# A Mamba-2 scan feeding a float32 MLP on one core: decoding ahead of a lagging gate, and all scan scores in one group

## The chip, the cores and the metric

One core of one Trainium2 chip runs the kernel. The metric is device time in microseconds (us), the median of several executions. Five engines run at once, each with its own queue that is worked off in order: TensorE (PE in the profile, with its weight loads shown as PEld), VectorE (DVE), ScalarE (ACT), GpSimd (POOL) and SyncE (SP), which here only starts DMA transfers.

## What is computed

Two parts, one after the other. The first is a chunked state-space scan over `x` [4, 8, 768, 32] with decays `a` and projections `B` and `C` [4, 8, 768, 16]; per chunk and per (batch, head):

```python
cum = np.cumsum(la, axis=-1)                       # la = log(clip(a))
L = np.exp(cum[:, :, :, None] - cum[:, :, None, :]) * causal
CB = np.einsum('bhin,bhjn->bhij', Cc, Bc)          # the scores
y_intra = np.einsum('bhij,bhjd->bhid', CB * L, xc)
y_inter = np.einsum('bhin,bhnd->bhid', Cc, state) * decay_to_i[:, :, :, None]
state = decay_full * state + sum_j(Bx)             # carried to the next chunk
```

The second takes the scan's result as 3072 tokens of 256 values and computes `h = x @ w_in` (256 to 2048), `g = h * clip(h + 3, 0, 6) / 6` and `g @ w_out` (2048 to 256). The two weights arrive as float64, so the kernel decodes them to float32 on the chip.

## The kernel before

**Blocks and tiles.** The 768 steps are cut into NC = 6 blocks of 128 steps; with 4 batches a block has 512 tokens. Each block's MLP goes over NF = 16 tiles of 128 hidden units (f = 0 to 15). While the MLP of block k runs, the scan of block k + 1 is threaded between its tiles, since the next block's MLP needs its result.

**Block 0** uses the decoded weights directly in float32: per tile `first_full` (two products into a bank of PSUM, L654), `gate_full` (ACT L661, then DVE L662) and, five tiles later, `second` (four products with `Aacc`, L666; the same line serves all products of the helper `product`). Four PSUM banks (h0, h1, G0, G1) go round for the hidden tiles, so tile f + 4 needs that the gate of tile f has read its bank.

**Decoding** of a weight piece (eight pieces, four of each weight; `decode`) is five steps of a generator: (a) ACT copies the top 16 bits, L194; (b) DVE L211, L213, L197; (c) ACT L217; (d) ACT L219, DVE L201, and the load of a later piece; (e) DVE L225 and L231, which writes the piece `full`. The list `WEAVE` says which pieces take a step at tile f: in block 0 these steps stand in the DVE and ACT queues *behind* `gate_full(f)`.

**Blocks 1 to 5** split each float32 operand in two float32r parts and take three products each way. Per tile f: `follow` (four products, L666), `lead` of the next tile (two products, into the other of the banks h0, h1), `scale` (ACT L674, in place on that bank), `ramp` (ACT L701), `gate` (DVE L706), `g_high` (ACT L716), `g_low` (DVE L720), `g_gap` (POOL L725), and `second` of tile f - 2 (six products). The last two tiles of the last block take a float32 path of their own (`whole`, `gate_whole`, `second_whole`).

**Splitting the weights** into their parts (`split_w`, `split_o`; ACT L622/L641, DVE L624/L643, POOL L627/L646) happens piece by piece in blocks 0 and 1.

**The scan of one block**, in PE order: `into_state` (32 products, `sp`, L488), `scores` (`cb`, L477), `from_state` (L466) and `mix` (L536) into `yy`. A float32 product of these small shapes shows as two instructions in the trace. DVE multiplies the decays `L` with the scores (`weigh`, L509), `take` (ACT L504), `halfway` and `renew` (DVE L498, L525) form the state, and `y_high`, `y_gap`, `y_low` (ACT L602, DVE L605, L610) write the next MLP's input. Scores, `from_state` and `mix` are done in two rounds, one for each half of the heads (u = 0, 1), because all of them pass through the same pair of banks, "xy".

**Preparing the scan.** SP loads `B` and `C` as `pairs` (L90, 16 transfers), `x`, and the running sums for `L` and `eto`; POOL masks L (`conceal`, L156), adds (`add_cum`, L370), makes `bs` (`ends`, L390); DVE turns B and C (`turn_squares`, L439), and makes `cT` and `csT` (`part_heads` L446, `fade` L452). The block's output is turned by DVE (L768) and stored with 32 transfers (L774).

**Order.** It is written out by hand: `at(t, slot, fn, ...)` books work for step t = 16 k + f and a slot of that step (mid, ramp, gate, act, low, pool, late, pe, end), and the loop calls `go(t, slot)` at fixed places. Each engine's queue therefore has the order in which the loop meets the calls.

Of the kernel before, what the change touches and what calls it, by code (L numbers as in the profile page):

```python
# [8 lines left out]
FP32 = mybir.dt.float32  # L9
# [5 lines left out]
ALU = mybir.AluOpType  # L15
# [6 lines left out]
def kernel(  # L22
# [507 lines left out]
    def mix(c, u, start=(False, False), batches=range(NB)):  # L530
        xt = xts[c]
        for b in batches:
            for h in range(u * HU, (u + 1) * HU):
                for a, rows in enumerate(HALF):
                    d0 = D * (h % HU)
                    nc.tensor.matmul(  # L536
                        out=ys[c][a, u][d0:d0 + D, b], lhsT=xt[rows, b * NH + h],
                        rhs=Ls[c][rows, b, h], start=(start[a] and b == 0), stop=True,
                        tile_position=(a * HT, d0), skip_group_check=True)
# [11 lines left out]
    def mix_first():  # L551
# [3 lines left out]
        for u in range(2):  # L555
            mix(0, u, (u == 0, True))
# [10 lines left out]
    def scan_scores(c, u):  # L567
        cb = bank("cb", [2, NB, 2, HT], "xy")
        cbs[c] = {2 * u + t: cb[:, t] for t in range(2)}
        scores(c, (2 * u, 2 * u + 1))  # L570
# [3 lines left out]
    def added(c, batches):  # L574

        if c not in sps:
            both = bank("sp", [2, TB], "xy")
            sps[c] = [both[:, a, :NB * 2 * D].rearrange("p (b d) -> p b d", b=NB)
                      for a in range(2)]
        into_state(c, batches)  # L580

    def from_states(c, u):

        both = bank("yy", [2, TB], "xy")
        yall[c, u] = both[:, :, :NB * HT]
        ys.setdefault(c, {}).update(
            {(a, u): yall[c, u][:, a].rearrange("p (b i) -> p b i", b=NB) for a in range(2)})
        for a in range(2):
            from_state(c, a, (2 * u, 2 * u + 1), start=True)

    def own(c, u, batches):
        mix(c, u, batches=batches)
# [37 lines left out]
    def split_o(i):  # L630
# [15 lines left out]
        nc.gpsimd.tensor_tensor(out=lo_, in0=w, in1=hi_, op=ALU.subtract)  # L646
# [233 lines left out]
    def plan_turned(c, t):  # L880
        at(t, "low", turn_squares, bcs[c][1], turned(c)[0])
        at(t + 1, "low", turn_squares, bcs[c][0], turned(c)[2])
        at(t + 2, "gate", part_heads, c)
        at(t + 2, "low", fade, c)

    def plan_round(c, u, t):
        at(t, "pe", scan_scores, c, u)
        at(t + 1, "gate", weigh, c, (2 * u,))
        at(t + 1, "low", weigh, c, (2 * u + 1,))
        at(t + 2, "pe", from_states, c, u)  # L890
        at(t + 2, "pe", own, c, u, (0,))
        at(t + 3, "pe", own, c, u, range(1, NB))
        at(t + 4, "ramp", y_high, c, u)
        at(t + 4, "gate", y_gap, c, u)
        at(t + 4, "gate", y_low, c, u)

    def plan_scan(c, t):
        at(t, "mid", added, c, range(3))
        at(t + 1, "pe", added, c, range(3, NB))
        at(t + 2, "ramp", take, c)  # L900
        at(t + 2, "gate", halfway, c)
        plan_round(c, 0, t + 2)
        at(t + 5, "low", renew, c)
        plan_round(c, 1, t + 7)

    def plan_parts(gen, t):
        at(t, "act", next, gen)
        at(t + 1, "low", next, gen)
        at(t + 1, "late", next, gen)

    SPLITS = [split_w(0), split_o(0), split_w(1), split_w(2), split_o(1), split_w(3),
              split_o(2), split_o(3)]
    for n, gen in enumerate(SPLITS):
        plan_parts(gen, (10, 12, 14, 16, 18, 21, 23, 25)[n])


    WEAVE = ["1", "114", "44", "442", "22", "225", "55", "55", "33", "33", "36",
# [8 lines left out]
    at(4, "pe", turn, 1)  # L926
    at(5, "pe", added, 1, range(NB))
    at(6, "gate", take, 1)
    at(6, "gate", halfway, 1)
    for u in range(2):  # L930
        t = (6, 10)[u]
        at(t, "pe", scan_scores, 1, u)
        at(t + 1, "gate", weigh, 1, (2 * u, 2 * u + 1))
        at(t + 1, "pe", from_states, 1, u)
        at(t + 2, "mid", own, 1, u, range(2))
        at(t + 2, "pe", own, 1, u, range(2, NB))
        at(t + 3, "ramp", y_high, 1, u)
        at(t + 3, "gate", y_gap, 1, u)
        at(t + 3, "gate", y_low, 1, u)
    at(8, "low", renew, 1)  # L940
    at(5, "pe", load_bc, 2)
    at(6, "pe", rows, 2)
    at(10, "pe", load_x, 2)
    plan_factors(2, 9)
    for f in range(NF):
        first_full(f)
        go(f, "mid")
        go(f, "ramp")
        gate_full(f)
        go(f, "gate")  # L950
        for i in WEAVE[f]:
            weights(int(i), 1)
        go(f, "act")
        go(f, "low")
        go(f, "pool")
        go(f, "late")
        if f >= BEHIND:
            second(0, f - BEHIND)
        go(f, "pe")
# [5 lines left out]
    for k in range(1, NC):  # L965
        t0, c = NF * k, k + 1
        if c < NC:
            s0 = t0 + 2
            plan_scan(c, s0)
            if c + 1 < NC:  # L970
                at(t0, "pe", rows, c + 1)
                at(s0 + 2, "pe", load_bc, c + 1)
                at(s0 + 11, "pe", load_x, c + 1)
                s1 = s0 + NF
                plan_factors(c + 1, s1 - (7 if k < 2 else 9))
# [98 lines left out]
```

## Time and profile before

| What | Value |
|---|---|
| Median of 3 runs | 381.92 us (381.5, 381.92, 383.69) |
| The profiled execution: its own time / its span | 379.74 us / 377.3 us |
| Busy share of the span: PE, DVE, ACT, POOL | 92%, 66%, 60%, 49% |
| Mean granted TensorE clock | 0.984 |
| Chain that ended last: PE, DVE, ACT, POOL | 65%, 16%, 8%, 4% |
| Costliest wait: POOL L725 for DVE gl L720 | 98.7 us in 54 waits |
| DMA moved | 25.13 MB, mean 67 GB/s |

Span is the time from the first to the last instruction; 2.4 us lie around it. Matmuls are pipelined, so a busy PE is not a PE at its peak: what a tile costs is read from the distance between equal instructions of one tile and the next. Groups in the profile name what is written, then what is read (`Aacc<-g,full`), and a line number of the kernel.

### The profile page before, as it was taken

The numbers are of one execution on the slowest core, as the hardware profiler recorded it, in microseconds if no ns is written. First come the engines' busy times: TensorE is split into PE (matmuls) and PEld (weight loads), VectorE is DVE, ScalarE is ACT, GpSimd is POOL, SyncE is SP. The second block draws the span as 40 slices with busy tenths as digits, with TensorE's granted clock in tenths as the row PEclk, the third lists the DMA queues.
The fourth block names the chain that finished last, engine by engine and source line by source line (L and its number), as shares of the span: only waits on it lengthen the run. The fifth ranks groups of instructions, "written<-read, shape, count | busy, mean of one in ns | idle before, by whom it ended". The sixth has DMA issues, their size and how long they took to land.

```text
span 377.3 us, 7999 instructions
## 1 busy us (share of the span) xinstructions
PE 347.7 (92%) x3148; PEld 241.9 (64%) x3148; DVE 250.8 (66%) x370; ACT 226.5 (60%) x388; POOL 184.7 (49%) x157
## 2 busy tenths in 40 slices
PE   6796889899997989879999999999999999999995
PEld 2552344433565757647777877777877777878882
DVE  6768667877388797786465785574867664465442
ACT  4676545687475655665556765465765555666661
POOL 2303001480466769984349954369844243445440
PEclk9999599999999999999999999999999999999998
DMA  7999466555001241900241911243201100002101
GB/s 162 213 269 204 132 142 149 128 70 126 0 3 22 33 67 35 181 5 11 33 60 40 169 30 20 34 65 64 21 2 30 28 2 3 0 7 32 20 0 56
DMA packets 94180, 25.13 MB, mean 67 GB/s; under 512 B 86784, under 2 KB 90528, under 8 KB 93632
## 3 DMA queue, kind: packets, MB, share of 16 engines
q1 hardware_dynamic: 89760, 23.33, 32.4%
q10 hardware_dynamic: 4384, 1.31, 1.5%
q8 instruction: 24, 0.39, 0.4%
q14 instruction: 12, 0.10, 0.1%
HBM read 21.33 MB, written 3.29 MB: 65 GB/s over the span
## 4 chain that ended last, share of the span: by engine, by line
PE 65%; DVE 16%; ACT 8%; POOL 4%; issue 4%; DMA 3%; SPq 0%; ACTq 0%; DVEq 0%; POOLq 0%
PE h L666 24%; PE Aacc L666 20%; PE Gacc L666 7%; PE h L654 5%; DVE gl L720 3%; PE cb L477 3%; PE yy L466 3%; POOL gg L725 2%; DVE g L706 2%; ACT gh L716 2%; PE yy L536 2%; ACT g L661 2%; DMA raw<-in_moe_w_in_dram 2%; ACT g L701 1%; DVE full L231 1%
## 5 line engine op out<-in xcount | busy, mean ns | idle before, releaser
L725 POOL TENSOR_TENSOR gg<-gh,gl 128x512 fp32r<-128x512 f32 x78 | 108.5, 1391 | 108.7 <-DVE gl L720 98.7
L701 ACT ACTIVATE g<-h,ramp_bias 128x512 f32<-128x512 f32 x78 | 53.7, 688 | 69.1 <-PE h L666 68.2
L720 DVE SCALAR_TENSOR_TENSOR gl<-gh,g 128x512 fp32r<-128x512 f32 x78 | 64.3, 824 | 42.8 <-ACT gh L716 38.9
L706 DVE SCALAR_TENSOR_TENSOR g<-g,h 128x512 f32<-128x512 f32 x78 | 53.3, 683 | 46.8 <-ACT g L701 46.4
L716 ACT ACTIVATE gh<-g 128x512 fp32r<-128x512 f32 x78 | 49.3, 633 | 36.8 <-DVE g L706 36.4
L666 PE MATMUL Aacc<-gh,oparts 128*128 128x512 f32 x156 | 62.0, 397 | 1.9 <-DVE stage L762 1.8
L666 PE MATMUL Gacc<-gg,oparts 128*128 128x512 f32 x156 | 61.6, 395 | 1.1 <-POOL gg L725 0.9
L666 PE MATMUL Aacc<-gl,low 128*128 128x512 f32 x156 | 61.1, 392 | 1.5 <-POOL low L646 1.5
L666 PE MATMUL h<-yp,w_high 128*128 128x512 f32 x160 | 54.1, 419 | 0.1
L666 PE MATMUL h<-yp,w_gap 128*128 128x512 f32 x160 | 51.1, 400 | 1.9 <-DVE g L706 1.9
L666 PE MATMUL h<-yp,low 128*128 128x512 f32 x160 | 49.9, 393 | 0.0
L674 ACT ACTIVATE h<-h 128x512 f32<-128x512 f32 x80 | 47.2, 591 | 0.0
L666 PE MATMUL Aacc<-g,full 128*128 128x512 f32 x72 | 36.0, 628 | 4.3 <-DVE full L231 4.3
L156 POOL TENSOR_SCALAR_AFFINE_SELECT L<-L 64x1024 f32<-64x1024 f32 (+1 forms) x16 | 22.0, 1378 | 29.6 <-DMA L<-cum_d 29.2
L666 PEld LDWEIGHTS h<-yp,w_gap 128*128 128x128 f32 x160 | 29.7, 188 | 10.5 <-DVE g L706 3.5
L666 PEld LDWEIGHTS Aacc<-gh,oparts 128*128 128x128 f32 x156 | 29.3, 188 | 9.4 <-DVE stage L762 2.7
L666 PEld LDWEIGHTS Gacc<-gg,oparts 128*128 128x128 f32 x156 | 29.3, 188 | 9.1 <-POOL gg L725 2.4
L666 PEld LDWEIGHTS Aacc<-gl,low 128*128 128x128 f32 x156 | 29.3, 188 | 8.5 <-POOL low L646 1.9
L666 PEld LDWEIGHTS h<-yp,low 128*128 128x128 f32 x160 | 30.0, 188 | 7.1
L666 PEld LDWEIGHTS h<-yp,w_high 128*128 128x128 f32 x160 | 27.6, 188 | 9.5 <-issue 2.3
L654 PE MATMUL h<-y,full 128*128 128x512 f32 x64 | 32.3, 637 | 1.1 <-DVE full L231 1.1
L666 PEld LDWEIGHTS Aacc<-g,full 128*128 128x128 f32 x72 | 14.0, 201 | 21.4 <-issue 17.5
(121 smaller groups left out, 411.9 us busy)
## 6 DMA issues: line engine op xcount, KB each, us to landing
raw<-in_moe_w_out_dram SPq DMA_DIRECT2D x4, 1024.0 KB
L<-cum_d SPq DMA_DIRECT2D x8, 512.0 KB
xt<-in_x_dram SPq DMA_DIRECT2D x6, 512.0 KB
raw<-in_moe_w_in_dram SPq DMA_DIRECT2D x3, 1024.0 KB
out_dram<-back SPq DMA_DIRECT2D x160, 16.0 KB
pairs<-in_C_dram SPq DMA_DIRECT2D x40, 32.0 KB
eto<-cum_e SPq DMA_DIRECT2D x20, 64.0 KB
B<-in_B_dram SPq DMA_DIRECT2D x5, 256.0 KB
```

Of the source, the lines that this page charges most:

```text
L156: nc.gpsimd.affine_select(out=t[rows], in_=t[rows], pattern=pattern, compare_op=ALU.is_ge, fill=-1e5, base=base, channel_multiplier=-1)
L466: nc.tensor.matmul(out=ys[c][a, q // 2][d0:d0 + 2 * D, b], lhsT=state[pair, b], rhs=csT[pair, b, HALF[a]], start=(start and b == 0), stop= ...
L477: nc.tensor.matmul(out=cbs[c][q][rows, b], lhsT=bT[pair, b, rows], rhs=cT[pair, b, :, rows], start=(b == 0), stop=True, tile_position=(32 ...
L536: nc.tensor.matmul(out=ys[c][a, u][d0:d0 + D, b], lhsT=xt[rows, b * NH + h], rhs=Ls[c][rows, b, h], start=(start[a] and b == 0), stop=True ...
L654: nc.tensor.matmul(out=h, lhsT=full[f // FP][:, j, f % FP * P:(f % FP + 1) * P], rhs=yps[0][:, j], start=(j == 0), stop=(j == NK - 1))
L666: nc.tensor.matmul(out=out_, lhsT=w, rhs=y, start=start, stop=True, skip_group_check=True)
L674: nc.scalar.mul(hs[k, f], hs[k, f], -1.0 / UP)
L701: nc.scalar.activation(g, hs[k, f], AF.Relu, bias=ramp_bias, scale=UP * UP / 6.0 / Z)
L706: nc.vector.scalar_tensor_tensor(out=g, in0=g, scalar=UP / Z, in1=hs.pop((k, f)), op0=ALU.min, op1=ALU.mult)
L716: nc.scalar.mul(gs[k, f][1], g, CUT * Z)
L720: nc.vector.scalar_tensor_tensor(out=low_, in0=high, scalar=-1.0 / Z, in1=g, op0=ALU.mult, op1=ALU.add)
L725: nc.gpsimd.tensor_tensor(out=gap, in0=high, in1=low_, op=ALU.subtract)
```

## The change

The words given with the change are: block 0 decodes ahead of a gate lagging a step; all scores in four banks at once; C and B turned by VectorE; last two tiles' second product in float32. Of these, `turn_squares` and the `whole` path stand in the kernel before as well; the diff moves the first in time and does not touch the second.

1. **Block 0.** The loop now runs to f = 16; at step f the decode steps of `WEAVE[f]` stand ahead of the gate of tile f - 1. `WEAVE` begins one step earlier.
2. **Scores.** All four pairs of heads are scored at once, into two banks of the hidden tiles and the two of "xy". In block 0 these are G0 and G1, at step 9. In blocks 1 to 4 there is one special step, f = 6: no `lead` of the next tile ahead of it, then gate, `second` of tile 4, all scores in banks h1 and h0, the four `weigh`, `second` of tile 5, then `lead` and `scale` of tiles 7 and 8.
3. **The rest of the scan.** `own` does `from_state` and `mix` in two groups, the first for half 0 of the steps with heads u = 0 and half 1 with u = 1, the second crosswise; a tiny ACT copy (`settle`) stands between them. `into_state` is no longer cut in two.
4. **Bookings.** Turning C and B moves from steps 14, 15, 16 to 11, 12, 13, and the masks and decays with them; `load_x` to step 9; in block 1 the stores of block 0 move from steps 3, 4 to 11, 14.
5. **Splits.** The last operation of `split_o(2)` and `split_o(3)` moves from POOL to DVE, and several splits are booked a step or two later.

```diff
-    def mix(c, u, start=(False, False), batches=range(NB)):
+    def mix(c, us, start=(False, False)):
...
+                    u, h, d0 = us[a], us[a] * HU + n, D * n
...
+    def all_scores(c, *tags):
+        own_ = [bank("cb", [NB, 2, HT], t) for t in tags]
+        both = bank("cb2", [2, NB, 2, HT], "xy")
+        cbs[c] = own_ + [both[:, t] for t in range(2)]
+        scores(c, range(NQ))
...
+    def own(c, us):
...
+        for a, u in enumerate(us):
+            from_state(c, a, (2 * u, 2 * u + 1), start=(us == (0, 1)))
+        mix(c, us)
...
+    def settle(c):
+        nc.scalar.copy(out=spare, in_=yall[c])
...
-        nc.gpsimd.tensor_tensor(out=lo_, in0=w, in1=hi_, op=ALU.subtract)
+        engine = nc.vector if i > 1 else nc.gpsimd
+        engine.tensor_tensor(out=lo_, in0=w, in1=hi_, op=ALU.subtract)
...
+    def plan_scan(c, t, slot, e):
+        at(t, slot, added, c)
+        at(t + 1, "ramp", take, c)
+        at(t + 1, "gate", halfway, c)
+        at(t + 2, "low", renew, c)
+        special[e] = c
+        at(e + 1, "pe", own, c, (0, 1))
+        at(e + 2, "ramp", settle, c)
+        at(e + 3, "pe", own, c, (1, 0))
+        plan_y(c, e + 4)
+    for gen, t, u, v in (
+            (split_w(0), 10, 11, 11), (split_o(0), 12, 13, 13), (split_w(1), 14, 15, 15),
+            (split_w(2), 16, 17, 17), (split_o(1), 18, 20, 20), (split_w(3), 21, 23, 23),
+            (split_o(2), 22, 24, 25), (split_o(3), 25, 28, 29)):
...
-    WEAVE = ["1", "114", "44", "442", "22", "225", "55", "55", "33", "33", "36",
+    WEAVE = ["114", "144", "4", "422", "22", "225", "55", "55", "33", "33", "36",
...
+    at(9, "mid", all_scores, 1, "G0", "G1")
+    at(9, "gate", weigh, 1, range(NQ))
+    at(10, "pe", own, 1, (0, 1))
+    at(11, "ramp", settle, 1)
+    at(12, "pe", own, 1, (1, 0))
+    plan_y(1, 13)
...
+    for f in range(NF + 1):
+        if f < NF:
+            first_full(f)
+            go(f, "mid")
+            for i in WEAVE[f]:
+                weights(int(i), 1)
+        if f:
+            gate_full(f - 1)
...
-                at(s0 + 2, "pe", load_bc, c + 1)
-                at(s0 + 11, "pe", load_x, c + 1)
-                s1 = s0 + NF
-                plan_factors(c + 1, s1 - (7 if k < 2 else 9))
+                at(t0 + 4, "pe", load_bc, c + 1)
+                at(t0 + 9, "pe", load_x, c + 1)
+                plan_factors(c + 1, t0 + 10)
...
-            at(t0 + 3 + m, "low", store, k - 1, m)
+            at(t0 + (11 + 3 * m if k == 1 else 3 + m), "low", store, k - 1, m)
...
-                plan_turned(c + 1, s1 - 4)
+                plan_turned(c + 1, t0 + 11, t0 + 12, t0 + 13)
...
+            skip = t in special
+            if skip:
+                ramp(k, f)
+                gate(k, f)
...
+                second(k, f - 2)
+                scan = special.pop(t)
+                all_scores(scan, *(f"h{(f + n) % 2}" for n in (1, 2)))
+                weigh(scan, range(NQ))
+                g_gap(k, f)
+                second(k, f - 1)
+                for n in (1, 2):
+                    lead(k, f + n)
+                    scale(k, f + n)
```

## The prediction, made before the changed kernel was run

> **What bounds the kernel now.** I read the page's busy shares first, then the sums by stage, cut at the first `follow` of each block (97.4, 159.0, 215.6, 269.5, 322.9 us), then the timeline inside the slow stages. Columns: length; busy us of PE, PEld, DVE, ACT, POOL; PE clock; DMA share; GB/s.
>
> ```profile
> 22.60:97.40 74.80, 66.23 (x451) 30.14 (x451) 52.90 (x74) 46.46 (x76) 19.74 (x15) 0.93 0.66 135
> 97.40:159.00 61.60, 55.77 (x510) 40.31 (x509) 47.94 (x57) 37.61 (x68) 43.87 (x29) 1.00 0.30 49
> 159.00:215.60 56.60, 53.98 (x513) 41.04 (x512) 37.92 (x54) 34.48 (x60) 37.86 (x35) 1.00 0.30 51
> 215.60:269.50 53.90, 53.16 (x513) 41.41 (x512) 35.31 (x55) 33.59 (x58) 34.44 (x30) 1.00 0.29 46
> 269.50:322.90 53.40, 52.67 (x511) 41.01 (x511) 33.48 (x54) 31.36 (x54) 23.06 (x19) 1.00 0.07 11
> 322.90:377.30 54.40, 49.50 (x210) 38.24 (x208) 26.46 (x42) 30.74 (x53) 19.97 (x16) 0.98 0.10 20
> ```
>
> PE sets the pace in blocks 3 and 4: a plain tile takes 2.78 us (the chain of waits has equal products at 213.01 and 215.79), 16 of them 44.4 us, and the scan's inserts the other 9.5. Blocks 1 and 2 are 7 and 2.7 us longer for the same work. Block 0 is 74.8 us long with 8.6 us of idle PE, and part of it ran at half clock:
>
> ```profile
> 38.00:42.00 4.00, 3.75 (x4) 1.18 (x4) 2.12 (x6) 2.94 (x5) 0.00 (x0) 0.50 0.58 223
> 42.00:46.00 4.00, 3.27 (x67) 2.10 (x68) 3.96 (x5) 2.49 (x3) 0.00 (x0) 0.50 0.23 19
> ```
>
> Why PE waits there (the timeline of all engines: start, us, engine, line; in brackets the idle time before and its releaser):
>
> ```profile
> 34.00 0.69 DVE L662 SCALAR_TENSOR_TENSOR g<-g,h 128x512 f32<-128x512 f32 x1 [1.25 <-ACT g L661]
> 34.61 1.32 DVE L201 SCALAR_TENSOR_TENSOR wm<-raw,wm 128x1024 f32<-128x1024 uint32 x1
> 35.85 0.90 DVE L225 TENSOR_TENSOR wse<-wse 128x1024 uint16<-128x1024 uint16 x1
> 36.78 1.32 DVE L231 SCALAR_TENSOR_TENSOR full<-wm,wse 128x1024 f32<-128x1024 f32 x1
> 38.24 3.75 PE L666 MATMUL Aacc<-g,full 128*128 128x512 f32 x4 [2.85 <-DVE full L231]
> ```
>
> The decode (L201 to L231) stands behind a gate that waits for its own product; PE then waits 2.85 us for the weight, and its next four products take 3.75 instead of 1.72 us.
>
> **Block 0.** PE's work by rows: 30 groups of four products at 1.72 (16 first, 14 second) 51.6; `lead` 0.5, turning 0.9, `sp` 1.1, scores 2 x 1.03, `from_state` 2 x 1.07, `mix` 4 x 0.38, eight switches at 0.1: 60.6. So 14.2 us are lost, about 4.0 of them to the half clock. In the new order I laid the queues side by side with these rows (L194, L217, L219 about 1.07 each; L211 to L197 1.5; L201 and L231 1.2; L225 0.7; gate halves 0.69). Piece 1 is ready at 28.3 instead of 30.8, but the gate of tile 0 now stands behind three decode steps of piece 4 and ends at 31.4: tile 4, which takes its bank, waits 1.8 us. Piece 4 is ready at 35.2 (before 38.1), its tile waits 0.3. Piece 2 is ready at 41, piece 5 at 49, piece 3 at 60, all ahead of need; pieces 6 and 7 (70, 81) are just in time. The loads behind them come earlier, since each waits for an L201: 35.99 to about 33, 44.42 to 38.6. New waits: the scores at step 9 need bank G1, which the gate of tile 7 leaves at 52.5 (1.5 us), and tile 10 needs G0, free when the first `weigh` is done (0.8). With 0.2 more, 4.6 us of waits. The scores' group falls from 2.06 to 1.13 us:
>
> ```profile
> 14.74 1.20 PE L477 MATMUL cb<-cT,bT 32*64 32x128 f32 x64 [1.94 <-DVE cT L446]
> ...
> 177.93 1.10 PE L477 MATMUL cb<-cT,bT 32*64 32x128 f32 x32 [0.51 <-ACT gh L716]
> ```
>
> The first scan already scores all four pairs at once, 64 instructions in the time of 32. Block 0: 60.6 - 0.9 + 4.6 = 64.3 for 74.8: **-10.5**. The longest wait is 1.8 us, so I count no half clock. Without that cover: +4.0.
>
> **Blocks 1 to 4, the inserts.** Before, from tile distances above 2.78: `sp` 1.17 + 0.37 + 0.1; scores 1.81 + 1.13 + 0.2; `yy` 2 x 2.38; together 9.5. After: `sp` in one group 1.45. The special step costs 1.13 + 0.1 for the scores, 0.36 for the gate of tile 6 (ramp, gate, two hand-overs 1.75 us, under a `second` of 1.39), and 0.45 for `scale` of tile 7 (0.59 plus hand-overs, under a `lead` of 0.47): 2.05. Four `weigh` (2.6) end before `own` needs them. `own` 2 x (1.07 + 0.87 + 0.2). `settle` is bounded by 0 and 0.4 (the `adds` copy, L504, 0.37) on an ACT that is idle 40%; I take 0. Together 7.8: **-1.75 per block**.
>
> **Blocks 1 to 3, what the bookings add.** The turning of C and B now meets the `y` work: steps 10 to 13 have no insert on PE to cover it, 11.1 us, and DVE gets 2.8 (two gate halves, two y parts) + 3.85 (the same and a turn, 1.09) + 2.45 + 3.1 (two cT 1.0, fade 0.68) = 12.2. And the turned tile must have landed:
>
> ```profile
> 229.84 15.91 SPq L774 DMA_DIRECT2D out_dram<-back  x32
> 245.85 0.40 SPq L83 DMA_DIRECT2D B<-in_B_dram  x1
> 246.29 6.70 SPq L90 DMA_DIRECT2D pairs<-in_C_dram  x8
> 253.03 4.62 SPq L90 DMA_DIRECT2D pairs<-in_B_dram  x8
> ```
>
> On SP's queue the 32 stores of a block, first issued 4.6 us into tile 3, stand ahead of B and C; the last packet lands 29.5 us after the first store (259.4). In blocks 2 and 3 that is 44 us after the block's start (tile 3 at 9.8, + 4.6 + 29.5); tile 11 begins at 38.4 (11 x 2.78 + 7.8) and DVE gets to the turn 4.6 later, at 43.0. It waits about 0.9, all gates behind it wait too, `lead` of tile 14 starts 0.9 late, the next two 0.4 and 0.2; 0.5 more for POOL, whose masks and adds (20 us of work with its L725 in six tiles of 16.7) are in the same steps. **+2.0 each.** In exchange block 2 loses its old 2.7 us of waits (turning and `fade` at 161 to 167). Block 2: 53.9 - 1.75 + 2.0 = 54.15 for 56.6, **-2.45**; block 3 54.15 for 53.9, **+0.25**; block 4, which prepares nothing, **-1.75**. In block 1 the stores go behind the loads, so B and C are early, but their turns (0.70 each) and `split_o(3)` (1.22 and 1.2) join DVE: steps 10 to 13 hold 15.2 us, and the last part of piece 7 comes 3.9 after tile 12's `second` wants it. With 0.8 for POOL and 0.5 at tile 4: 53.9 + 0.66 (two float32 seconds) - 1.75 + 5.2 = 58.0 for 61.6: **-3.6**. Block 5 and the tail: 0.
>
> Moving two `low` operations from POOL (L646, 2.37 alone) to DVE has a price on both: a DVE instruction with two SBUF inputs and a POOL instruction take turns:
>
> ```profile
> 134.82 1.21 DVE L643 SCALAR_TENSOR_TENSOR oparts<-oparts,full 128x1024 fp32r<-128x1024 f32 x1
> ...
> 135.06 2.12 POOL L725 TENSOR_TENSOR gg<-gh,gl 128x512 fp32r<-128x512 f32 x1 [2.98 <-DVE gl L720]
> ```
>
> L725 takes 1.30 alone and 2.12 here. The two moved operations may each wait out one L725 (0 to 1.3); I take 0 and keep 2.6 as a rival. [...]
>
> **Sum.** -10.5 - 3.6 - 2.45 + 0.25 - 1.75 = -18.05. The profiled execution's own 379.74 becomes 361.7 (span 359.25); it lies 0.57% under the median, so on 381.92 the forecast is **363.9 us**.
>
> **Rivals.** (A) Blocks 1 to 3 run clean: C and B land sooner or DVE has slack; -9 of the 9.2 charged: **354.9**. For it: their waits hang on margins of about 1 us. (B) ACT, not DVE, holds block 0: at step 10 it waits for `eto` and the mask of L (landing at about 62.6 by the old distances), and the gates behind it are late; half the idle stays, +6: **369.9**. (C) The moved splits wait for POOL: +2.6, **366.5**. (D) The clock halves again. One PE gap of 2.85 us gave 10.24 us at 0.5; dense tiles lose 5.1 in that. If the gap stays in block 0 (+4.0) and the DVE waits of blocks 1 to 3 each come as one gap over 2.85 (+15.3), it ends at **383.2, slower**. It decides from gaps near 2.85; I reckon with 0.9 to 1.8, only block 1 is near. [...] (E) The change does less than it says: in banks shared with hidden tiles the 64 scores run as slowly as two groups, 5 x 0.93: **368.5**; the first scan speaks against it.
>
> **Numbers.** Forecast 0.56, A 0.18, B 0.11, C 0.07, D 0.05, E 0.03. The forecast's own spread is 359 to 369; the range takes in A and B: 353.5 to 372. About 0.5% (1.9 us) is what a measurement here can tell from no change: faster 0.92, same 0.03, slower 0.05.
>
> **What would show it.** Right: no 0.50 in PE's clock around 38 to 47; no wait of PE for `full` over 0.5 us but a wait of tile 4 for a gate; `cb` x64 in 1.1 to 1.2 us; block 0 near 64, blocks 2 and 3 near 54, block 4 near 51.7; DVE's `bT` waiting for `pairs` in blocks 2 and 3. Wrong: gaps of PE moved to step 10 of block 0 (B), blocks 2 and 3 at 52 (A), any new 0.50 (D).

## The result, and the profile after

| | Before | After |
|---|---|---|
| Median (4 runs each, one session) | 382.37 us (381.5 to 383.69) | 378.24 us (377.65 to 379.16) |
| Ratio after / before, 95% interval | | 0.9891 [0.9855, 0.9928] |
| Profiled execution: own time / span | 379.74 / 377.3 us | 378.26 / 376.5 us |

The kernel is faster by about 1.1%, where 4.7% was forecast; 378.24 us lies outside the range of 353.5 to 372. The stages show where the rest went. This is the sum by stage of the changed kernel, cut again at the first `follow` of each block (columns as in the prediction):

```profile
23.60:91.10 67.50, 61.16 (x449) 28.57 (x450) 54.81 (x72) 45.88 (x77) 19.08 (x15) 0.97 0.74 149
91.10:160.00 68.90, 58.18 (x510) 42.42 (x509) 51.64 (x63) 38.11 (x70) 44.22 (x32) 0.93 0.17 25
160.00:215.00 55.00, 52.58 (x514) 40.03 (x512) 36.34 (x54) 33.11 (x59) 30.76 (x28) 1.00 0.49 87
215.00:270.10 55.10, 52.68 (x513) 40.16 (x513) 36.92 (x55) 33.17 (x59) 33.70 (x30) 1.00 0.25 35
270.10:322.60 52.50, 51.46 (x513) 40.57 (x514) 32.43 (x50) 32.16 (x57) 25.34 (x22) 1.00 0.08 11
322.60:376.50 53.90, 49.05 (x207) 37.81 (x205) 26.09 (x41) 30.47 (x52) 19.41 (x15) 1.00 0.10 20
```

Block 0 won 7.3 of the 10.5 us forecast. Block 1 **lost** 7.3 us (61.6 to 68.9) where 3.6 were to be won: it is now the longest stage, with 10.7 us of idle PE and a mean clock of 0.93. Blocks 2 to 4 are each 0.9 above the forecast. From here on line numbers are those of the changed kernel: L663 `first_full`, L670/L671 `gate_full`, L675 `product`, L715 `gate`, L725 `g_high`, L729 `g_low`, L734 `g_gap`; L632 and L635 are the DVE and POOL operations of `split_w`, L651 and L655 the last two of `split_o`.

**Block 0.** The old gap at 35.4 us is gone, and so is the half clock behind it. A new gap stands late in the block (timeline of all engines):

```profile
65.17 0.63 ACT L384 ACTIVATE eto<-eto 128x512 f32<-128x512 f32 x1 [8.23 <-DMA eto<-cum_e]
68.39 0.69 DVE L671 SCALAR_TENSOR_TENSOR g<-g,h 128x512 f32<-128x512 f32 x1 [5.98 <-ACT spare L600]
70.37 3.20 POOL L635 TENSOR_TENSOR w_gap<-w_high,low 128x1024 fp32r<-128x1024 f32 x1 [3.91 <-DVE low L632]
71.27 2.85 DVE L225 TENSOR_TENSOR wse<-wse 128x1024 uint16<-128x1024 uint16 x1
74.16 1.32 DVE L231 SCALAR_TENSOR_TENSOR full<-wm,wse 128x1024 f32<-128x1024 f32 x1
75.53 0.94 PE L675 MATMUL Aacc<-g,full 128*128 128x512 f32 x1 [2.78 <-DVE full L231]
```

ACT waits 8.23 us for `eto` to land; the gates and the decode of piece 6 stand behind it in ACT's queue, so DVE idles 5.98 us (a gate waits for several things, and the one named last, L600, is a copy of 0.14 us that stood in ACT's late queue itself). L225 then runs beside GpSimd and takes 2.85 us (0.68 at 40.29), and PE waits 2.78 us for the decoded weight.

**Block 1.** Most of the loss is in tile 6, the special step: 13.20 us, against 7.58 in blocks 2 and 4. The same view there:

```profile
112.42 2.35 POOL L655 TENSOR_TENSOR low<-full,oparts 128x1024 fp32r<-128x1024 f32 x1
112.66 2.66 DVE L729 SCALAR_TENSOR_TENSOR gl<-gh,g 128x512 fp32r<-128x512 f32 x1 [0.76 <-ACT gh L725]
114.82 0.50 PE L675 MATMUL Aacc<-gl,low 128*128 128x512 f32 x1 [2.46 <-POOL low L655]
115.69 1.51 DVE L498 SCALAR_TENSOR_TENSOR state<-adds,parity,later 128x128 f32<-128x128 f32 x2
117.13 0.67 DVE L715 SCALAR_TENSOR_TENSOR g<-g,h 128x512 f32<-128x512 f32 x1
117.86 1.55 PE L477 MATMUL cb<-cT,bT 32*64 32x128 f32 x43 [1.25 <-DVE g L715]
```

GpSimd's `low` of `split_o(1)`, now booked for step 20, ends at 114.8; PE has wanted it for 2.46 us. DVE's `g_low` beside it takes 2.66 us instead of 0.69 (such a stretching beside GpSimd is called the lock from here on), `renew` (L498) stands behind that, the gate of tile 6 behind `renew`, and the scores, which take the gate's bank, wait another 1.25 us. Then the clock (windows of 3.4 us):

```profile
113.40:116.80 3.40, 1.79 (x7) 1.04 (x7) 3.37 (x3) 0.75 (x2) 2.67 (x2) 1.00 0.26 59
116.80:120.20 3.40, 2.34 (x63) 2.01 (x64) 1.98 (x5) 1.58 (x2) 0.78 (x1) 0.50 0.09 22
120.20:123.60 3.40, 3.40 (x9) 2.63 (x9) 2.19 (x4) 0.00 (x0) 0.49 (x1) 0.50 0.00 0
```

After a stretch in which PE was busy 1.79 of 3.40 us it runs at 0.50 for 6.83 us. Tile 10 has a wait of 1.56 us (for the `low` of `split_o(2)`), tile 14 waits of 1.31 and 2.43 us (a gate; the `low` of `split_o(3)`), and 3.41 us at half clock:

```profile
154.51 0.80 PE L675 MATMUL Aacc<-gl,low 128*128 128x512 f32 x1 [2.43 <-DVE low L655]
```

**The rest.** All 64 score instructions take 1.21 us (at 53.83), as forecast. Behind a block's stores the order on SP's queue is as before, and `bT` follows 30.2 us after the first store (first SP's queue, the stores and the last of `pairs`):

```profile
229.14 16.59 SPq L783 DMA_DIRECT2D out_dram<-back  x32
...
252.33 4.62 SPq L90 DMA_DIRECT2D pairs<-in_B_dram  x8
```

And DVE's timeline, the turn that reads it, after 0.66 us of idle time whose releaser the trace does not name:

```profile
259.33 1.11 DVE L439 STREAM_TRANSPOSE bT<-pairs 128x512 f32<-128x512 f32 x1 [0.66 <-issue]
```

### The profile page after: what moved, and what is told of

It is laid out like the page before. It is cut to its first block, busy times and chain, and to the rows that moved or that the text cites. A ratio compares the mean times of both kernels' runs of the same rounds, so it can differ in the third digit from the quotient of the medians.

```text
span 376.5 us, 8016 instructions
## 1 busy us (share of the span) xinstructions
PE 343.1 (91%) x3148; PEld 240.0 (64%) x3148; DVE 255.5 (68%) x372; ACT 225.2 (60%) x393; POOL 178.3 (47%) x155
## 3 DMA queue, kind: packets, MB, share of 16 engines
q10 hardware_dynamic: 4384, 1.31, 1.6%
## 4 chain that ended last, share of the span: by engine, by line
PE 36%; SPq 7%; DVE 7%; ACT 4%; DMA 2%; issue 2%; POOL 1%; ACTq 0%; POOLq 0%; DVEq 0%
PE h L675 16%; PE Aacc L675 11%; PE Gacc L675 5%; SPq L783 4%; SPq L90 3%; DVE g L715 2%; DMA L<-cum_d 2%; DVE gl L729 2%; ACT gh L725 1%; DVE cT L446 1%; ACT g L710 1%; PE yy L466 1%; POOL gg L734 1%; PE yy L537 1%; DMA pairs<-in_B_dram 1%
## 5 line engine op out<-in xcount | busy, mean ns | idle before, releaser
L734 POOL TENSOR_TENSOR gg<-gh,gl 128x512 fp32r<-128x512 f32 x78 | 107.5, 1379 | 120.0 <-DVE gl L729 112.1
L729 DVE SCALAR_TENSOR_TENSOR gl<-gh,g 128x512 fp32r<-128x512 f32 x78 | 63.7, 816 | 47.2 <-ACT gh L725 42.5
L725 ACT ACTIVATE gh<-g 128x512 fp32r<-128x512 f32 x78 | 49.3, 631 | 56.1 <-DVE g L715 55.2
L715 DVE SCALAR_TENSOR_TENSOR g<-g,h 128x512 f32<-128x512 f32 x78 | 53.2, 681 | 42.8 <-ACT g L710 42.5
L710 ACT ACTIVATE g<-h,ramp_bias 128x512 f32<-128x512 f32 x78 | 53.4, 685 | 44.3 <-PE h L675 44.1
L675 PE MATMUL Aacc<-gl,low 128*128 128x512 f32 x156 | 62.7, 402 | 6.5 <-DVE low L655 4.0
L675 PE MATMUL Aacc<-gh,oparts 128*128 128x512 f32 x156 | 62.7, 402 | 1.0 <-ACT stage L763 0.7
L675 PE MATMUL Gacc<-gg,oparts 128*128 128x512 f32 x156 | 62.7, 402 | 0.0
L675 PE MATMUL h<-yp,w_gap 128*128 128x512 f32 x160 | 51.2, 406 | 4.3 <-DVE g L715 4.3
L675 PE MATMUL h<-yp,w_high 128*128 128x512 f32 x160 | 53.2, 413 | 1.4 <-ACT h L683 1.0
L675 PE MATMUL h<-yp,low 128*128 128x512 f32 x160 | 50.3, 396 | 0.0
L675 PEld LDWEIGHTS h<-yp,w_gap 128*128 128x128 f32 x160 | 30.0, 191 | 15.0 <-DVE g L715 7.8
L675 PEld LDWEIGHTS Aacc<-gl,low 128*128 128x128 f32 x156 | 29.8, 191 | 14.4 <-DVE low L655 4.9
L675 PE MATMUL Aacc<-g,full 128*128 128x512 f32 x72 | 35.1, 619 | 3.2 <-DVE full L231 3.2
L675 PEld LDWEIGHTS h<-yp,w_high 128*128 128x128 f32 x160 | 28.7, 190 | 13.4 <-ACT h L683 6.1
L675 PEld LDWEIGHTS Aacc<-gh,oparts 128*128 128x128 f32 x156 | 29.7, 190 | 9.5 <-ACT stage L763 1.1
L675 PEld LDWEIGHTS h<-yp,low 128*128 128x128 f32 x160 | 30.2, 189 | 7.0
L675 PEld LDWEIGHTS Gacc<-gg,oparts 128*128 128x128 f32 x156 | 29.9, 191 | 6.5
L663 PE MATMUL h<-y,full 128*128 128x512 f32 x64 | 30.2, 604 | 1.5 <-DVE g L671 1.4
L156 POOL TENSOR_SCALAR_AFFINE_SELECT L<-L 64x1024 f32<-64x1024 f32 (+1 forms) x16 | 20.0, 1252 | 24.5 <-DMA L<-cum_d 24.0
L675 PEld LDWEIGHTS Aacc<-g,full 128*128 128x128 f32 x72 | 13.7, 194 | 19.7 <-issue 15.2
```

The source lines that it names most:

```text
L156: nc.gpsimd.affine_select(out=t[rows], in_=t[rows], pattern=pattern, compare_op=ALU.is_ge, fill=-1e5, base=base, channel_multiplier=-1)
L663: nc.tensor.matmul(out=h, lhsT=full[f // FP][:, j, f % FP * P:(f % FP + 1) * P], rhs=yps[0][:, j], start=(j == 0), stop=(j == NK - 1))
L675: nc.tensor.matmul(out=out_, lhsT=w, rhs=y, start=start, stop=True, skip_group_check=True)
L710: nc.scalar.activation(g, hs[k, f], AF.Relu, bias=ramp_bias, scale=UP * UP / 6.0 / Z)
L715: nc.vector.scalar_tensor_tensor(out=g, in0=g, scalar=UP / Z, in1=hs.pop((k, f)), op0=ALU.min, op1=ALU.mult)
L725: nc.scalar.mul(gs[k, f][1], g, CUT * Z)
```

## The experiments

Theories after the first reading: in block 1 parts arrive late for the steps they are now booked to (**late parts**), and the waits halve the clock. Rival: DVE and GpSimd are too full in block 1 for any booking (**full engines**). All runs at a glance: lengths of blocks 0 to 4 in the profiled execution (from first `follow` to first `follow`), then the median and the ratio to the kernel before in the same session.

| Kernel | 0 | 1 | 2 | 3 | 4 | us | ratio, 95% |
|---|---|---|---|---|---|---|---|
| before | 74.8 | 61.6 | 56.6 | 53.9 | 53.9 | 382.37 | 1 |
| after | 67.5 | 68.9 | 55.0 | 55.1 | 52.5 | 378.24 | 0.9891 [0.9855, 0.9928] |
| splits_early | 67.5 | 65.3 | 55.1 | 55.3 | 52.5 | 375.12 | 0.9835 [0.9776, 0.9895] |
| eto_first | 64.2 | 68.9 | 54.9 | 55.2 | 52.5 | 376.37 | 0.9865 [0.9800, 0.9930] |
| turn_late | 65.9 | 67.9 | 53.4 | 54.8 | 53.8 | 376.75 | 0.9879 [0.9817, 0.9942] |
| busy_gap | 69.0 | 68.7 | 55.1 | 55.1 | 52.5 | 377.04 | 0.9897 [0.9831, 0.9964] |
| block0_only | 69.0 | 63.0 | 56.6 | 53.9 | 53.9 | 373.71 | 0.9850 [0.9808, 0.9892] |
| splits_fit | 67.2 | 63.1 | 55.1 | 55.1 | 52.5 | 372.70 | 0.9822 [0.9764, 0.9880] |
| turn_in_hole | 69.3 | 68.0 | 53.4 | 54.3 | 53.4 | 375.56 | 0.9887 [0.9832, 0.9942] |
| all_three | 66.3 | 62.3 | 54.9 | 54.3 | 53.4 | 369.54 | 0.9737 [0.9688, 0.9786] |
| rest_only | 72.7 | 68.7 | 54.9 | 55.2 | 52.5 | 384.42 | 1.0081 [1.0050, 1.0113] |
| renew_late | 64.3 | 58.9 | 54.8 | 54.3 | 53.4 | 367.23 | 0.9616 [0.9584, 0.9648] |
| lows_on_pool | 66.1 | 60.7 | 54.8 | 54.3 | 53.4 | 369.04 | 0.9677 [0.9643, 0.9710] |
| busy_all | 66.0 | 65.4 | 55.3 | 56.0 | 52.5 | 375.75 | 0.9845 [0.9771, 0.9918] |
| factors_early | 66.1 | 61.4 | 54.6 | 53.1 | 52.8 | 365.90 | 0.9581 [0.9517, 0.9645] |
| best | 64.2 | 60.1 | 54.5 | 53.1 | 52.8 | 364.45 | 0.9558 [0.9492, 0.9625] |
| best_10 | 64.1 | 58.3 | 54.1 | 53.1 | 52.8 | 363.70 | 0.9529 [0.9495, 0.9562] |

### Which part of the change wins, which loses

**block0_only**: `before` with the loop `for f in range(NF + 1)` and the new WEAVE, nothing else. **rest_only**: the changed kernel with the old loop and the old WEAVE.

> The kernel before with the new loop and WEAVE of block 0 alone (decoding ahead of the gate that lags a step); the scan in two rounds, the old splits and bookings stay. Theory (the parts add up): block 0 falls from 74.8 to 67 to 69 us, as in the changed kernel, with the wait for eto at its end; block 1 stays at about 61.6, blocks 2 to 5 at 56.6, 53.9, 53.9, 53.9. The time is about 375.5, below the changed kernel's 378.2, because the changed kernel gives 7.3 us back in block 1. Rival: block 0's gain needs the single group of scores (two rounds are two more waits for a gate that lags): block 0 stays above 71 us, the time above 378.

> The complement of block0_only: the changed kernel with the old loop and WEAVE in block 0 (decode steps behind a gate that does not lag); everything else as changed. Theory (the parts add up): block 0 is 73 to 75 us again, block 1 stays at 68 to 69 and blocks 2 to 5 as in the changed kernel; the time is about 385, slower than the kernel before by 0.5 to 1%, since the rest of the change loses 7 us in block 1 and gains 2 in blocks 2 to 4. Rival: block 1's loss hangs on what block 0 leaves behind (the state of the queues, when the loads land): then block 1 is near 61.6 here and the time near 380.

Both nearly as the theory had it (block 0 of `rest_only` took 72.7 us, not 73 to 75). The new order of block 0 alone is worth 1.5% of the time; the rest of the change alone is slower than the kernel before by 0.8%. Together that is 0.7%, against the 1.1% measured for the whole. By their ratios `block0_only` (0.9850) looks better than the changed kernel (0.9891), but the two intervals overlap. The parts of `rest_only` show it once more: block 1 at 68.7 us, whatever block 0 leaves behind. In `block0_only` block 1 took 63.0, 1.4 more than expected: scores that waited 2.22 us and 3.41 us of half clock.

### Late parts, or full engines

**splits_early**:

```diff
-            (split_w(2), 16, 17, 17), (split_o(1), 18, 20, 20), (split_w(3), 21, 23, 23),
-            (split_o(2), 22, 24, 25), (split_o(3), 25, 28, 29)):
+            (split_w(2), 16, 17, 17), (split_o(1), 18, 19, 19), (split_w(3), 21, 22, 22),
+            (split_o(2), 23, 24, 24), (split_o(3), 25, 26, 26)):
```

> The changed kernel with the second and third operation of split_w(3), split_o(1), split_o(2) and split_o(3) booked one step behind the first, as in the kernel before (19, 22, 24, 26; split_o(2) starts at step 23 again). Theory (late parts): in block 1 TensorE's waits of 2.46, 1.56 and 2.43 us at tiles 6, 10 and 14 are for the low parts of the output weight, which the new bookings deliver too late, and two of them halve the clock for 6.83 and 3.41 us. Then tile 6 falls from 13.2 to about 7.9 us, tile 10 from 4.72 to about 3.1, tile 14 from 8.09 to about 3.8: block 1 from 68.9 to about 58, the time to about 367. Rival (full engines): VectorE and GpSimd have too much to do in block 1 whatever the booking, so the waits only move to other tiles: block 1 stays above 65, the time above 374.

By its numbers the rival's outcome came (block 1 above 65, the time above 374), but the trace is in between: no wait of PE for a `low` is left in block 1, but gates on DVE took their place (1.60 us at tile 5, 1.51 at tile 6, 2.96 at tile 12, the last one with 3.41 us of half clock). Block 1 is 65.3. Both theories hold a part. **splits_fit** puts the splits where DVE has room:

```diff
+            (split_o(1), 16, 17, 17), (split_w(2), 18, 20, 20), (split_w(3), 21, 22, 22),
+            (split_o(2), 22, 23, 24), (split_o(3), 24, 25, 25)):
```

> The changed kernel with other bookings of the splits, placed where VectorE has room: split_o(1) at 16, 17, 17 and split_w(2) at 18, 20, 20 (swapped), split_w(3) 21, 22, 22, split_o(2) 22, 23, 24, split_o(3) 24, 25, 25. Theory (late parts and a full VectorE, both): what moving the splits one step ahead only shifted (it left 4.63 us at tile 5, 9.36 at tile 6, 3.58 at tile 10, 7.21 at tile 12) comes from VectorE's steps 19, 26 and 27; with split_o(3) in step 25, which the own products stretch by 1.8 us, and split_w(2) as the late one, no wait over 1.5 us is left in block 1, its clock is not halved, and block 1 falls from 68.9 to about 58.5: the time to about 368. Rival (full engines): VectorE and GpSimd are full in block 1 as a whole; block 1 stays above 64, the time above 373.

63.1, between the two theories (58.5, or above 64): tiles 10 to 14 lost their long waits (1.11 us is the longest left), but tile 6 still took 12.04 us. **all_three** adds the edits of `eto_first` and `turn_in_hole` (below).

> The changed kernel with three edits at once: eto and L ahead of B and C in block 0, the splits placed as in splits_fit, the turns as in turn_in_hole. If the three causes are independent: block 0 64.2 (as measured with eto ahead), block 1 about 58, blocks 2 and 3 about 53, block 4 52.5, block 5 and the tail 53.9: span about 357 with the 23 us of the start, time about 359 to 361. If they share a cause (VectorE full), the sum is smaller: 366 to 370.

At 369.54 us the three gains do not add up to the 359 to 361 of independent causes. Tile 6 can be read cleanly here (all_three, timeline):

```profile
110.47 2.37 POOL L635 TENSOR_TENSOR w_gap<-w_high,low 128x1024 fp32r<-128x1024 f32 x1
110.70 2.68 DVE L729 SCALAR_TENSOR_TENSOR gl<-gh,g 128x512 fp32r<-128x512 f32 x1 [0.76 <-ACT gh L725]
...
113.75 1.49 DVE L498 SCALAR_TENSOR_TENSOR state<-adds,parity,later 128x128 f32<-128x128 f32 x2
115.17 0.67 DVE L715 SCALAR_TENSOR_TENSOR g<-g,h 128x512 f32<-128x512 f32 x1
115.90 2.01 PE L477 MATMUL cb<-cT,bT 32*64 32x128 f32 x62 [3.79 <-DVE g L715]
```

No part of a weight is late any more; the gate is. In a plain tile the `lead` of the next tile runs meanwhile; in the special step there is none, and PE waits 3.79 us. **renew_late**, on top of `all_three`, removes both things ahead of the gate, the locked `g_low` and `renew`:

```diff
-        at(t + 2, "low", renew, c)
+        at(t0 + 8 if k == 1 else t + 2, "low", renew, c)
...
-            (split_o(1), 16, 17, 17), (split_w(2), 18, 20, 20), (split_w(3), 21, 22, 22),
+            (split_w(2), 15, 15, 15), (split_o(1), 16, 17, 17), (split_w(3), 21, 22, 22),
```

> all_three with two more bookings changed in block 1: renew (two VectorE operations, 1.9 us, whose result nobody reads before step 29) goes from step 21 to step 24, and split_w(2) from 18, 20, 20 to 15, 15, 15. Theory (chain): in all_three the special step waits 3.79 us for its own gate, which on VectorE stands behind a g_low of 2.68 us (locked by GpSimd's L635) and renew; nothing can cover it, because the special step issues no product of a later tile ahead of it. With both gone the wait falls under 1 us, the clock is not halved, tile 6 falls from 12.9 to 7.6 to 8.2 us and block 1 from 62.3 to about 57.5: the time from 369.5 to about 364.5. Rival: the wait is the special step's own price in block 1 (VectorE full): tile 6 stays above 10 us, the time above 367.

Tile 6 is 7.42 us: the theory of the chain is right (renew_late, timeline; no wait ahead of the scores):

```profile
110.69 0.69 DVE L715 SCALAR_TENSOR_TENSOR g<-g,h 128x512 f32<-128x512 f32 x1 [0.84 <-ACT g L710]
111.00 1.62 PE L477 MATMUL cb<-cT,bT 32*64 32x128 f32 x64
```

The two were moved in one run, so their shares are not measured apart. Block 1 is 58.9 rather than 57.5, and the time 367.2 rather than 364.5, because `renew` and the splits now back up on DVE until tile 11 (a wait of 2.38 us).

### How much of it is the clock

**busy_gap** and **busy_all** leave every wait and fill it with dummy products:

```diff
+                if k == 1:
+                    busy(2, bank("d", [TB], f"h{(f + 1) % 2}"))
                 second(k, f - 2)
                 scan = special.pop(t)
+                if k == 1:                                # busy_all only
+                    busy(1, bank("d", [TB], f"h{(f + 1) % 2}"))
...
+                if (k, f) == (1, 14):                     # busy_all only
+                    busy(2, bank("d", [2, TB], "xy")[:, 0])
```

> The changed kernel with two dummy products (1.7 us of TensorE, into a free bank, never read) ahead of the one product that waits at tile 6 of block 1. The wait for the low part stays. Theory: an idle TensorE of about 2.5 us is what halves the clock; with at most 1.3 us of idle time left the 6.83 us at 0.5 from 116.8 on do not come, tile 6 falls from 13.2 to about 10.2 us and block 1 to about 66, the time by about 3 us. The later half clock at tile 14 stays (its wait is not filled). Rival: the clock follows something else, such as the small products of the scores: then it halves all the same and the time stays within 1 us.

> The changed kernel with dummy products (two of 0.86 us ahead of the wait for the low part and one ahead of the scores at tile 6, two ahead of the wait at tile 14 of block 1), never read; all waits stay as they are. Theory: with TensorE kept busy the clock is not halved at 117 and 154 us; tile 6 falls from 13.2 to about 11.3 us (7.58 and the waits of 2.46 and 1.25), tile 14 from 8.09 to about 6.5: block 1 from 68.9 to 65.4, so the clock is 3.5 of the 7.3 us lost there and the waits are the rest. Rival: the clock halves all the same, block 1 stays at 68 to 69 us.

`busy_gap` missed: the clock still halved, for 3.41 instead of 6.83 us, and block 1 did not get shorter by more than 0.3. One reason is that tile 14, whose waits were the same, now drew 6.83 us of half clock (from 153.5 us on) instead of 3.41, so that block 1 had 10.24 us at half clock in both kernels. With three waits filled (2.46, 1.25 and 2.43 us) there is no half clock, and block 1 is 65.4 us, the number expected: of the 7.3 us lost, 3.5 are clock; the other 3.8 are the waits, less what the inserts won.

### Block 0: who waits for eto

**eto_first**:

```diff
-    at(5, "pe", load_bc, 2)
-    at(6, "pe", rows, 2)
+    at(5, "pe", rows, 2)
+    at(6, "pe", load_bc, 2)
```

> The changed kernel with one swap in block 0: the loads of L and eto for block 2 (SP) are booked at step 5, ahead of B and C, which go to step 6. Theory: in block 0 ACT stands idle for 8.23 us until eto lands at 65.17, all gates and the decode of piece 6 behind it are late, TensorE waits 2.78 us at 72.75 and its clock is halved for 3.41 us. With the swap eto lands some 13 us earlier; block 0 falls from 67.5 to about 64 us, the time by 3 to 4 us to about 374.5. Rival: the decode of the last pieces is held by VectorE beside GpSimd (L225 took 2.85 us and L211 2.54 us there instead of 0.67 and 0.43): then the wait stays and the gain is under 1.5 us. Block 1 is not touched: 68 to 70 us by both.

The wait of PE for `full` at the end of block 0 is gone and block 0 is 64.2 us. Over all profiles the gain is smaller: the seven with `eto` behind (the changed kernel among them, `block0_only` and `rest_only` not) have a block 0 of 65.9 to 69.3, mean 67.5, the seven with `eto` ahead 64.1 to 66.3, mean 65.0, so 2.4 us. In both groups the clock makes the spread. Without a half clock in block 0 it took 65.9 and 66.0 us with `eto` behind (`turn_late`, `busy_all`) and 64.1 to 64.3 with `eto` ahead (four kernels); with one it took 67.2 to 69.3 and 66.1 to 66.3. So the wait for `eto` is worth about 1.7 us at full clock. The half clocks with `eto` ahead follow a wait ahead of the scores at 55 us (1.70 and 1.81 us, for a gate, as forecast) or one ahead of `sp` at 43 to 45 us (2.88 in `all_three`; 1.2 to 2.9 in these kernels), which the forecast did not have. The trace names no releaser for the latter (the changed kernel, timeline):

```profile
43.48 0.69 DVE L428 TENSOR_TENSOR csT<-t_ps,eto 128x512 f32<-128x512 f32 x1 [0.66 <-issue]
44.27 0.85 PE L488 MATMUL sp<-xt,bs 64*32 64x64 f32 x64 [1.75 <-issue]
```

But in all 16 profiles that show this wait, the kernel before among them, `sp` starts 0.10 or 0.11 us after the end of L428, the last to read `t_ps`, and the code puts `t_ps` and `sp` into the same banks "xy". L428 follows ACT's copies out of `t_ps`, which in the fourteen kernels of these two groups stand behind a decode step (L194). Where the wait is longest (`all_three`, `turn_in_hole`), that step itself waits 1.55 and 1.45 us for its raw piece to land.

### Blocks 2 and 3: DVE or GpSimd

**turn_late** books the turns at 14, 15, 16 again. **turn_in_hole** books them at 12, 13, 14, in the slot behind the gate (where DVE waits 0.76 us for ACT's `gh` anyway):

```diff
-                plan_turned(c + 1, t0 + 11, t0 + 12, t0 + 13)
+                plan_turned(c + 1, t0 + 14, t0 + 15, t0 + 16)     # turn_late
+                plan_turned(c + 1, t0 + 12, t0 + 13, t0 + 14)     # turn_in_hole
...
-        at(t, "low", turn_squares, bcs[c][1], turned(c)[0])
-        at(u, "low", turn_squares, bcs[c][0], turned(c)[2])
+        slot = "low" if c == 2 else "gate"
+        at(t, slot, turn_squares, bcs[c][1], turned(c)[0])
+        at(u, slot, turn_squares, bcs[c][0], turned(c)[2])
```

> The changed kernel with the turning of B and C back at steps 14, 15 and 16 of each block. Theory: the turns at steps 11 to 13 meet the y work on VectorE, and pairs has just landed there; that costs blocks 2 and 3 2.6 us each at tiles 13 to 15 (3.5, 3.7, 3.7 us and 3.8, 3.4, 3.7 instead of 2.79) and part of block 1's tile 14. Without it blocks 2 and 3 fall from 55.0 to about 52.5 us and block 1 by 1 to 2 us: the time to about 372. Rival: the same work only moves to the first tiles of the next block, where the kernel before lost 2.7 us in block 2 at tile 2 (6.12 us): the sum of blocks 2, 3 and 4 changes by less than 2 us, the time stays within 2 us of 378.

> The changed kernel with the turns of B and C (for blocks 3 to 5) booked at steps 12, 13, 14, and in the slot behind the gate instead of behind g_low. Theory: a tile's chain on VectorE is gate 0.6, a hole of 0.76 while ACT makes gh, g_low 0.6: an operation behind g_low must fit in 0.8 us of a 2.79-us tile, one behind the gate has the hole as well. By that sum the backlog after tile 14 falls from about 3 to about 1 us: blocks 2 and 3 fall from 55.0 to about 53 us each, block 4 stays at 52.5, block 1 loses up to 1 us: the time to about 373.5. Rival: C and B land too late or GpSimd is the one that is full: blocks 2 and 3 together fall by less than 1.5 us.

Both mostly moved the loss into the first tiles of the next block, as the rival of `turn_late` had it: the sum of blocks 2 to 4 is 161.9 and 161.2 us; in the changed kernel it is 162.5. **factors_early** moves GpSimd's share instead (`plan_factors(c + 1, t0 + 8)` on top of `renew_late`):

> renew_late with GpSimd's preparation of L, tmp and bs for the next block (the masks, the running sums, the decayed B) booked from step 8 instead of step 10. If GpSimd is the full engine at tiles 11 to 15 (two of L734's 1.3 us, an add of 1.04 to 1.49 and a bs of 0.4 to 0.87 in each tile): blocks 2 and 3 fall from 54.8 and 54.3 to about 53, block 4 from 53.4 to 52.6; the time by about 3 us to 364. If VectorE is the full one, they change by less than 0.7 us each, and the time stays within 1.5 us of 367.

Block 3 falls by 1.2 to 53.1 and block 4 by 0.6: with the turns in the hole, GpSimd was the full one there, and PE's waits for `gg` (0.50 and 0.35 us at tiles 15 and 0) are gone. Block 2 stays at 54.6, since its tile 0 takes 4.61 us behind block 1, and the time falls by 1.3 us rather than 3. In block 1 the same booking hurt: tile 10 took 7.68 us.

### The moved splits, and a better version

**lows_on_pool** puts the last operation of `split_o(2)` and `split_o(3)` back on GpSimd, on top of `renew_late`; **best** is `factors_early` with the splits spread once more; **best_10** moves GpSimd's preparation in block 1 back to step 10.

```diff
-        engine = nc.vector if i > 1 else nc.gpsimd
+        engine = nc.gpsimd                                # lows_on_pool
...
+            (split_o(1), 16, 17, 17), (split_w(3), 19, 20, 22),    # best, best_10
+            (split_o(2), 20, 22, 23), (split_o(3), 23, 24, 25)):   # best, best_10
...
-        at(v, "low" if v > u else "late", next, gen)
+        at(v, "low" if v > u and v != 22 else "late", next, gen)    # best, best_10
...
+                plan_factors(c + 1, t0 + (10 if k == 1 else 8))    # best_10
```

> renew_late with the last operation of split_o(2) and split_o(3) back on GpSimd, at the same steps. By the lock (two SBUF-reading VectorE operations wait for GpSimd's L734: 2.3 us instead of 1.2 in two runs) VectorE gets 2.4 to 3.5 us back and GpSimd gets 4.7 us more: if VectorE is the full one, block 1 falls by up to 2 us; if GpSimd's products gg come late instead, it rises by 1 to 3. I expect a difference of under 1.5 us in block 1, and nothing elsewhere.

> factors_early with the splits of block 1 spread once more: split_w(3) at 19, 20, 22, split_o(2) at 20, 22, 23, split_o(3) at 23, 24, 25, so that steps 23 to 25 hold four VectorE operations of 1.2 us less one and tile 11 finds no backlog. Expected if the wait of 2.38 us at tile 11 is VectorE's backlog: tile 11 falls from 5.42 to about 3.3 us, block 1 from 58.9 to about 56.5, 2 us less than factors_early, the time about 362. If it is the lock with GpSimd, the wait moves and block 1 stays above 58.

> best with GpSimd's preparation booked from step 10 in block 1 (as in the changed kernel) and from step 8 in blocks 2 and 3. If VectorE is held up by GpSimd's masks at tiles 8 and 9: tile 10 falls from 7.66 to about 3 us without a wait over 1.5 us, block 1 from 60.1 to 56 to 57 us, the time by about 3 us to 361. If the splits alone are too many there, tile 10 or 11 stays above 5 us and block 1 above 58.5.

With the two operations on GpSimd block 1 is 1.8 us longer, a little more than expected (PE waits 2.10 us for `gg` at tile 12): at these bookings the move to DVE was right. It is not free: beside an L734 the operation took 2.30 and 2.28 us in `splits_early`, and 1.22 and 1.21 in the changed kernel, where it started 0.2 us ahead of the L734, which then took 2.12 us. `best` did not shorten tile 10 (7.66), although DVE had less to do. The lock explains it (factors_early, timeline, tiles 8 and 9 of block 1):

```profile
123.16 2.69 POOL L156 TENSOR_SCALAR_AFFINE_SELECT L<-L 64x1024 f32<-64x1024 f32 x2
...
124.76 2.15 DVE L655 TENSOR_TENSOR low<-full,oparts 128x1024 fp32r<-128x1024 f32 x1
125.82 2.23 POOL L734 TENSOR_TENSOR gg<-gh,gl 128x512 fp32r<-128x512 f32 x1
126.84 1.49 DVE L525 TENSOR_TENSOR later<-mid,eto 128x256 f32<-128x256 f32 x1
128.01 2.54 POOL L156 TENSOR_SCALAR_AFFINE_SELECT L<-L 64x1024 f32<-64x1024 f32 x2
128.37 2.32 DVE L498 SCALAR_TENSOR_TENSOR state<-adds,parity,later 128x128 f32<-128x128 f32 x2
```

Three DVE operations that take 1.22, 0.41 and 0.61 us where no GpSimd instruction runs at their start take 5.96 together beside GpSimd's masks (L156) and the L734 between them. With GpSimd's preparation in block 1 back at step 10 (`best_10`) tile 10 is 2.87 us and block 1 58.3 (expected 56 to 57; a wait of 1.39 us for `gg` at tile 13 is left). It runs in 363.7 us (median; 361 was expected) and beats both kernels; its profiled execution, the fastest of five at 361.31 us, has no half clock between 7 and 358 us.

## Why the prediction was wrong, step by step

The lengths by stage, forecast and measured: start 22.6 / 23.6, block 0 64.3 / 67.5, block 1 58.0 / 68.9, block 2 54.15 / 55.0, block 3 54.15 / 55.1, block 4 51.65 / 52.5, the rest 54.4 / 53.9. The miss of 17.25 us in the span is 63% block 1.

- **Block 1, -3.6: the step that failed.** It priced the special step at 2.05 us in every block and put the waits into steps 10 to 13. Against block 4, which has neither splits nor preparation, tile 6 took 5.6 us more, where nothing was charged, and tiles 10 to 15 took 8.7 more, where 4.7 were; some 3.5 us of this is half clock. The price holds where the engines are free: tile 6 took 7.58 us in blocks 2 and 4, and 7.42 in block 1 once the chain ahead was clear. In the changed kernel it took 13.20, since two things were not laid against it: `split_o(1)` was booked from step 19 to 20, on GpSimd behind L734, for a `second` that comes one `lead` earlier than before; and `renew` stood on DVE directly ahead of the gate that nothing covers. The forecast named the wait for the last part of piece 7 (3.9 us): it came, at tile 14, as 2.43.
- **"The longest wait is 1.8 us, so I count no half clock."** That was said of block 0, and even there it is no safe rule: in `factors_early` a wait of 1.70 us ahead of the scores was followed by 3.41 us of half clock. For block 1 the clock stood only in rival D, with its threshold read off a single gap of 2.85 us. The halving came after waits of 2.46 and 1.25 us in tile 6 and 1.31 and 2.43 in tile 14: 3.5 us. This is what D describes, in blocks 0 and 1, on the faster side.
- **Block 0, -10.5: measured -7.3.** With `eto` ahead four kernels came within 0.2 us of the forecast (64.1 to 64.3 in `eto_first`, `renew_late`, `best`, `best_10`); the other three, with a half clock, took 66.1 to 66.3. In `eto_first` the waits of tile 4 (1.41 us, 1.8 forecast) and for piece 4 (0.38, 0.3) came as laid out, but the total is partly luck: the 1.5 us at the scores did not come, and 1.34 us ahead of `sp`, which the forecast did not have, stood in their place. Rival B, with 0.11, is what happened, at 3.2 us instead of 6, and about half of that is the clock. Its own landing time (62.6) was 2.6 early.
- **Blocks 2 and 3, +2.0 each: the loss was there and its place right, its owner half right.** Tiles 13 to 15 took 10.9 us instead of 8.4, so +2.5 (rival A, without these waits, is out). DVE was charged 1.5 and GpSimd 0.5; the runs showed that clearing DVE alone won 1.5 in block 2 and 0.8 in block 3, part of it given back in block 4, and that GpSimd's masks and adds two steps earlier won another 1.2 in block 3.
- **Block 4, -1.75: measured -1.4** against its own start. The forecast cut it 0.5 us before its first `follow`, which it gave to block 5. `sp` and the scores came as priced (64 scores in 1.21 us: rival E is out), and `settle` took ACT 0.14 us.
- **The lock (rival C, +2.6 against the 0 taken): 0 was right in this order** (1.22 and 1.21), and 1.1 for each in another (2.30, 2.28). But the same lock hit other instructions that were priced at their bare times: `g_low` 2.66 us (0.69 alone), `renew` 1.51 (0.61), L225 2.85 (0.68). The price was looked for at the moved operations and not at their neighbours.

## What to carry to other kernels

When a step gives up the work that covered a wait (here the `lead` ahead of the special step), list everything queued ahead of what it then waits for, on each engine, in every block in which it runs: the block with extra work sets the price, not the clean one. Book work that is not urgent (`renew`, read 8 steps later) away from such a step. Measure the parts of a combined change alone: here one part was worth 1.5% and the other cost 0.8%.

## What the runs showed of the hardware

**Half clock followed stretches in which PE worked 0.52 of the time or less.** In the profiles of the kernel before and of the changed kernel the changes of the granted clock are multiples of 3.41 us (10.24 / 3) apart: half clock for 10.24 us from 37.48 in the one, for 3.41, 6.83 and 3.41 us from 75.84, 116.80 and 154.35 in the other, and at the end of both runs. I cut both profiles into stretches of 3.41 us along these changes and added up PE's busy time in each. From 24 us on 198 stretches had the full clock. Six of them were followed by half clock: one with a busy share of 0.39 in the kernel before, three with 0.19, 0.52 and 0.28 in the changed one, and the last stretch of each run, where PE's work runs out (0.23 and 0.03). Of the 192 that were followed by full clock, one had a share of 0.49 (changed kernel, from 41.71 us), all others 0.57 or more. So in these two profiles a low share in one such stretch goes with the half clock behind it, and the two groups overlap (0.49 and 0.52). In the stretch ahead of the 6.83 us (113.39 to 116.80) PE worked 1.79 us, and parts of the two waits of tile 6, of 2.46 and 1.25 us, lie in it.

The longest wait alone did not tell the cases apart. In `factors_early` a wait of 1.70 us ahead of the scores, ending at 55.21 us, was followed by half clock: the next four products took 3.31 us, where four take 1.88 at full clock. In `turn_in_hole` a wait of 2.40 us, ending at 76.94, was not: the next four took 1.98.

**The lock, in numbers.** In the same two profiles `g_low`, which reads two tiles in SBUF, took 0.67 to 0.69 us in the 105 cases in which no GpSimd instruction ran at its start, and 0.68 to 2.69 us in the 51 in which one did (2.67 at 137.39 us in the kernel before). The gate, whose `h` lies in PSUM, took 0.65 to 0.70 us in 116 such cases. The stretching reached 16-bit work as well: L225, with two inputs in SBUF, took 2.85 us at 71.27 beside GpSimd's L635 (0.68 alone), and L211, with one, 2.54 us at 75.99 beside L655 (0.42 alone).
